# Sums by tensor_reduce, a list that keeps two engines off each other's time, and first-row scores ranked first

## The chip, the cores and the metric

The kernel runs on one core of a Trainium2 chip. The metric is the device time of one execution in microseconds (us). A core has five engines that run their own queues: TensorE (PE in the profile; its weight loads are PEld), VectorE (DVE), ScalarE (ACT), GpSimd (POOL) and SyncE (SP, which here only issues DMAs). They meet through semaphores.

## The reference, cut to what matters

Attention with a threshold comes first, for 8 batches of 8 heads with 576 positions of 64 numbers; then a mixer with a token and a channel part. The mixer's weights are 64-bit floating-point numbers.

```python
scores = (1 / 8) * q @ k.T                       # per batch and head, 576 x 576
thresh = max(scores, axis=-1) - tau
scores = where(scores >= thresh, scores, -1e9)
attn   = exp(scores - max(scores))
attn   = attn / (sum(attn) + 1e-09)
x      = (attn @ v) as (batch, position, head * 64)

h  = relu(x.T @ w_tok1) @ w_tok2                 # tokens:   576 -> 256 -> 576
u  = x + h.T
out = u + relu(u @ w_ch1) @ w_ch2                # channels: 512 -> 1536 -> 512
```

## The kernel before, in words

A **row** is one batch: four pairs of heads. A **unit** is 128 query positions of a pair with both heads, and a **round** is two units. A row has 9 rounds; there are 72 rounds in all, so rounds 0 to 8 are row 0 (in the code `it < UB // 2`, with `UB = 18`).

A round goes through the engines like this. TensorE computes scores of both units into the only two PSUM tiles for scores (`scores_of_two`, L729), so the next round's scores wait for this round's Prelus. VectorE takes four maxima (`top`, L742). GpSimd turns each into a bias (`shift`, L747). ScalarE writes four masked tiles by Prelu (`mask`, L757), then four exponentials with their sums (`exps`, L767; the sum comes out of an accumulator). VectorE adds 1e-9 to the unit's two sums and inverts them (`inverse`, L272 and L273). GpSimd scales the tile by them (`scale`, L280). In row 0 TensorE turns the tile by nine transposes in three banks (`turn`, L295), and VectorE or ScalarE copies each bank out (`turned`, L300); in later rows VectorE and DMAs do the turning (`turn_blocks`, L310, and `move`, L322). TensorE multiplies with the values (`values`, L360 and L365) into a bank that is copied to `xT` (L369). There are four tiles `e`, so a Prelu also waits for the unit four back to be turned. Queries and keys of the next pair are turned by VectorE (`prep`, L265).

The four mixer weights come as 64-bit words and are converted on the chip in 31 pieces: 7 of the token weights, 12 of the first and 12 of the second channel weight. A piece is loaded by a DMA into one of three raw places, ScalarE does two steps (`on_scalar`, L215 and L217), VectorE three (`on_vector`: part 0 at L225, part 1 at L227, part 2 at L231), and GpSimd adds (`on_gpsimd`, L239). Row 0's token part needs the first seven pieces and all of row 0's attention; its channel part needs the others (`ch1` at L834 the first 12, `ch2` at L850 all).

The order on every engine is written before the program runs, by a list (`Scheduler`). An operation has an engine, a planned cost, what it depends on and a rank. For every engine `pick` takes, of the operations that could start by the engine's planned clock, the one of lowest rank, then the oldest; where none could, the earliest. An operation may have an `other` engine with its own cost: whichever picks it first gets it. `start` says from when an operation could run: the planned ends of what it depends on with a lag, a free bank, and the engine's clock. Scores that have rank 1 are also held until as much of the mixer's work has been planned as `planned_at` says.

The ranks that the change touches or passes: scores 1, maxima and biases 0, Prelus 1, conversion steps 1 on ScalarE, 2 on VectorE and 1 on GpSimd, exponentials 2, inverse 2, scaling 1, turns, values and their copies 0, `prep` 3, token steps 1.5. After attention the rest of the channel part runs in a fixed order (L1192 and its neighbours), from about 980 us to the end.

Of the kernel before, what the change touches and what calls it, by code (L numbers as in the profile page):

```python
# [9 lines left out]
F32 = mybir.dt.float32  # L10
# [3 lines left out]
AF = mybir.ActivationFunctionType  # L14
ALU = mybir.AluOpType
AX = mybir.AxisListType

P = 128
# [3 lines left out]
def kernel(  # L22
# [25 lines left out]
    nc = tc.nc  # L48
    B, H, S, D = q.shape
# [19 lines left out]
    const = ctx.enter_context(tc.tile_pool(name="const", bufs=1))  # L69
    work = ctx.enter_context(tc.tile_pool(name="work", bufs=2))  # L70
    small = ctx.enter_context(tc.tile_pool(name="small", bufs=6))
# [15 lines left out]
    UB = 9 * NP // 2  # L87
# [128 lines left out]
            else:  # L216
                nc.scalar.activation(out=h2, in_=hi.bitcast(F32), func=AF.Abs)  # L217

    def on_vector(i, part):
        if wide(i):  # L220
            dst = pieces[i][0]
            lo, hi, h2 = raws[i]
            bits = dst.bitcast(U32)
            if part == 0:
                nc.vector.tensor_scalar(out=h2, in0=h2, scalar1=2.0**-15, scalar2=2.0**16, op0=ALU.max, op1=ALU.mult)  # L225
            elif part == 1:
                nc.vector.tensor_scalar(  # L227
                    out=bits, in0=h2.bitcast(U32), scalar1=3, scalar2=0, op0=ALU.logical_shift_left, op1=ALU.bitwise_or
                )
            else:  # L230
                nc.vector.scalar_tensor_tensor(  # L231
                    out=bits, in0=hi, scalar=0x80000000, in1=bits, op0=ALU.bitwise_and, op1=ALU.bitwise_or
                )
# [13 lines left out]
    tlow = const.tile([P, 1], F32, name="tlow")  # L247
    toff = const.tile([P, 1], F32, name="toff")
    ntau = const.tile([P, 1], F32, name="ntau")


    heads = {}
# [16 lines left out]
    def inverse(u):  # L269
        e, rs = st[u]  # L270
        rr = small.tile([P, 2], F32, tag="rr", name=f"rr_{u}")
        nc.vector.tensor_scalar(out=rr, in0=rs, scalar1=1e-9, scalar2=None, op0=ALU.add)  # L272
        nc.vector.reciprocal(out=rr, in_=rr)  # L273
        st[u] = e, rr

# [212 lines left out]
    class Op:  # L488

        def __init__(self, eng, cost, fn, deps, after, rank, lag, row, index):  # L490
            self.eng, self.cost, self.fn, self.rank, self.lag, self.row, self.index = eng, cost, fn, rank, lag, row, index
            self.end, self.bank, self.frees, self.later, self.open, self.other = None, None, None, [], 0, None
            self.dmas, self.landed = None, None
            self.deps = [d for d in deps if d is not None]
            for d in self.deps + [d for d in after if d is not None]:
                if d.end is None:
                    d.later.append(self)
                    self.open += 1
# [5 lines left out]
    class Scheduler:  # L504
# [5 lines left out]
            self.ready = {e: [] for e in self.clock}  # L510
            self.in_flight, self.moved = deque(maxlen=FLIGHT), 0.0

        def op(self, eng, cost, fn, deps=(), rank=5, lag=0.2, row=None, after=(), other=None, dmas=None):
            x = Op(eng, cost, fn, deps, after, rank, lag, row, len(self.ops))
            x.other, x.dmas = other, dmas
            self.ops.append(x)
            if not x.open:
                self.enter(x)
            return x
# [13 lines left out]
        def start(self, x, eng):  # L533
            t = max([d.landed or d.end + (d.lag if d.eng != eng else 0.0) for d in x.deps] + [0.0])
            if x.dmas and len(self.in_flight) == FLIGHT:
                t = max(t, self.in_flight[0])
            if x.bank:
                frees = [b.free for b in self.banks if b.free is not None]
                if not frees:
                    return None  # L540
                t = max(t, min(frees))
            return max(t, self.clock[eng])
# [68 lines left out]
    sched = Scheduler()  # L611
# [3 lines left out]
    def key_op(*key):  # L615
        return keyed.get(key)

    def put(key, x):
        keyed[key] = x
        return x  # L620
# [17 lines left out]
    def put_dv(i, part):  # L638
        before = key_op("pool", 26) if part == 1 and i >= CONV - 2 else None
        put(  # L640
            ("dv", i, part),
            sched.op(
                "dve",
                (0.46, 0.47, 0.62)[part],
                lambda: on_vector(i, part),
                (key_op("ac", i, 1), key_op("dv", i, part - 1), before),
                CR[2],
            ),
        )

# [64 lines left out]
    def scores_of_two(us):  # L715
        sc = [ps_s2.tile([P, 3, MAIN], F32, tag="sc", name=f"sc{h}_{us[0]}") for h in range(2)]
        for k, u in enumerate(us):
            b, p0, t = units[u]
            if t == SHARED:
                parts = [(b * NP + p0, slice(MAIN, S), slice(0, 64)), (b * NP + p0 + 1, slice(0, LAST), slice(64, P))]  # L720
            else:
                o = P * t if t < SHARED else LAST + P * (t - SHARED - 1)
                parts = [(b * NP + p0 + (t > SHARED), slice(o, o + P), slice(0, P))]
            for f in range(3):
                for n, cols, rows in parts:
                    for h in range(2):
                        r = slice(D * h, D * h + D)
                        qT, kT = heads[n]
                        nc.tensor.matmul(  # L729
                            sc[h][rows, f, HT * k : HT * k + HT],  # L730
                            lhsT=qT[r, cols],
                            rhs=kT[r, HT * f : HT * f + HT],
                            start=True,
                            stop=True,
                            skip_group_check=True,
                        )
            part = [sc[h][:, :, HT * k : HT * k + HT] for h in range(2)]
            st[u] = part, small.tile([P, 2], F32, tag="mx", name=f"mx_{u}"), small.tile([P, 2], F32, tag="bias", name=f"bias_{u}")

    def top(u, h):  # L740
        part, mx, _ = st[u]
        nc.vector.tensor_reduce(out=mx[:, h : h + 1], in_=part[h], axis=AX.XY, op=ALU.max)  # L742

    def shift(u, h):
        _, mx, bias = st[u]
        c = slice(h, h + 1)
        nc.gpsimd.tensor_scalar(out=bias[:, c], in0=mx[:, c], scalar1=toff, scalar2=-SCALE, op0=ALU.add, op1=ALU.mult)  # L747

    def mask(u, h):
        if h == 0:  # L750
            part, _, bias = st[u]
            rs = small.tile([P, 2], F32, tag="rs", name=f"rs_{u}")
            e = att.tile([P, 2 * S], F32, tag="e", bufs=4, name=f"e_{u}")
            masked[u] = e, rs, part, bias
        e, rs, part, bias = masked[u]
        eh = e[:, S * h : S * h + S].rearrange("p (f x) -> p f x", f=3)
        nc.scalar.activation(out=eh, in_=part[h], func=AF.Prelu, bias=bias[:, h : h + 1], scale=SCALE, alpha=STEEP)  # L757
        if h == 1:
            del masked[u]
            st[u] = e, rs  # L760
# [3 lines left out]
    def exps(u, h):  # L764
        e, rs = st[u] if u not in masked else masked[u][0:2]
        eh = e[:, S * h : S * h + S]
        nc.scalar.activation(out=eh, in_=eh, func=AF.Exp, bias=ntau, accum_out=rs[:, h : h + 1])  # L767


    UNITS = len(units)  # L770
# [1 line left out]
    SCORES, VALUES = 2.2, 3.45  # L772
# [202 lines left out]
    def make_round(it):  # L975
        us = (2 * it, 2 * it + 1)
        pre = [key_op("pre", u - 2, h) for u in us for h in range(2)]
        prepared = []
        for u in us:
            b, p0, t = units[u]  # L980
            n = b * NP + p0
            for m in [n] * (t <= SHARED) + [n + 1] * (t >= SHARED):
                prepared += [key_op("prep", m, 0) if it else None, key_op("prep", m, 1)]
                prepared += [key_op("prep", 0, "first")] if not it else []
        x = put(("S", it), sched.op("pe", SCORES, lambda: scores_of_two(us), pre + prepared, 1))
        row, k = divmod(it, UB // 2)
        x.plan = planned_at(row - 1, k) if row else -1.0
        for h in range(2):
            for u in us:
                put(("mx", u, h), sched.op("dve", 0.665, lambda u=u, h=h: top(u, h), (x,), 0))  # L990
                put(("bias", u, h), sched.op("pool", 0.24, lambda u=u, h=h: shift(u, h), (key_op("mx", u, h),), 0))
        for h in range(2):
            for u in us:
                deps = [key_op("bias", u, h)] + [key_op("mx", v_, h) for v_ in us]
                if h == 0:
                    deps += [key_op("T", u - 4), key_op("pre", u - 1, 0)]
                else:
                    deps.append(key_op("pre", u, 0))
                put(("pre", u, h), sched.op("act", 0.64, lambda u=u, h=h: mask(u, h), deps, 1, lag=0.25))
        for u in us:  # L1000
            b, p0, t = units[u]
            for h in range(2):
# [3 lines left out]
            deps = [s]  # L1006
            G = rank_of_group(b, p0, t // GU)
            if not b:
                deps += [key_op("V", G - 2) if t % GU == 0 else None, key_op("T", u - 1)]
                for third in range(3):  # L1010
                    x, y = sched.banked(
                        0.33,
                        lambda bank, u=u, third=third: turn(u, third, bank),
# [8 lines left out]
                    deps = [x]  # L1022
# [348 lines left out]
```

## Time and profile before

| | |
|---|---|
| median of 3 runs | 1346.2 us (1345.57 to 1347.57) |
| the profiled execution | 1346.21 us, its span 1344.3 us |
| mean granted TensorE clock | 0.975 of full speed |
| busy: PE, DVE, ACT, POOL | 1261.7, 802.1, 570.9, 354.2 us |
| conversions on VectorE | 11.6 to 144 us, 93 instructions |
| L272 and L273 (`inverse`) | 144 instructions each, 18.5 to 906 us |
| first token work of row 0's second half | 145.7 us |
| first L834, first L850 | 167.3 us, 206.8 us |

How it is read: busy time is the union of an engine's instructions; the slices cut the span into 40 equal parts; the chain of waits follows the last instruction back to what released it at each step. The timeline lists start, length, engine, line, operation, tiles and shapes, with the idle time before an instruction and its releaser in brackets. A line number is that of the kernel before.

### The profile page before, as it was taken

How to read it: one execution, taken by the hardware profiler on the slowest of the kernel's cores; microseconds unless marked ns; L12 is line 12 of the kernel's file. 1: busy time of each engine (PE TensorE's matmuls, PEld its weight loads, DVE VectorE, ACT ScalarE, POOL GpSimd, SP SyncE). 2: the span in 40 equal slices, each digit the busy share in tenths (PEclk: the TensorE clock that was granted, in tenths of full speed). 3: DMA queues.
4: the chain of work that ended last, by engine and by line, in shares of the span. 5: the costliest groups of instructions: out<-in, count | busy, mean ns of one | idle time of the engine just before them, and what ended most of it. 6: DMA issues, size and time to landing. Idle time of an engine off the chain costs nothing.

```text
span 1344.3 us, 21936 instructions
## 1 busy us (share of the span) xinstructions
PE 1261.7 (94%) x7982; PEld 1002.0 (75%) x7982; DVE 802.1 (60%) x1449; ACT 570.9 (42%) x1244; POOL 354.2 (26%) x658
## 2 busy tenths in 40 slices
PE   6778899999989999998999999899999999999998
PEld 5555579688657866875785776687988888888887
DVE  7899965384756766586576667665154443444352
ACT  6888654464644554455355537541020211112020
POOL 4666522142423323333233323320000000010100
PEclk7798899999989999999999999999999999999999
DMA  9655673463776575675667477173020211021011
GB/s 175 153 137 153 145 166 85 88 153 87 180 168 141 125 161 137 140 155 128 143 157 156 118 154 164 49 180 90 9 69 18 64 32 32 24 58 30 32 32 32
DMA packets 307194, 145.11 MB, mean 108 GB/s; under 512 B 206672, under 2 KB 299856, under 8 KB 307088
## 3 DMA queue, kind: packets, MB, share of 16 engines
q1 hardware_dynamic: 305216, 143.51, 46.3%
q8 instruction: 63, 1.03, 0.3%
q10 hardware_dynamic: 1872, 0.21, 0.1%
q14 instruction: 43, 0.35, 0.1%
HBM read 47.32 MB, written 13.50 MB: 45 GB/s over the span
## 4 chain that ended last, share of the span: by engine, by line
PE 58%; DVE 16%; SPq 10%; ACT 6%; DMA 6%; issue 3%; POOL 1%; DVEq 0%; ACTq 0%; POOLq 0%
PE o L1192 10%; PE bank L850 8%; PE bank L834 7%; SPq L322 6%; DVE mx L742 6%; PE hx L1192 6%; PE bank L365 5%; PE sc L729 5%; PE hz L1192 4%; PE oz L1192 4%; PE hmm L1192 4%; DVE T L310 3%; ACT e L757 3%; ACT e L767 2%; DMA eT<-T 2%
## 5 line engine op out<-in xcount | busy, mean ns | idle before, releaser
L757 ACT ACTIVATE e<-sc,bias 128x576 f32<-128x576 f32 x288 | 197.5, 741 | 223.6 <-DVE mx L742 180.8
L280 POOL TENSOR_SCALAR e<-e,rr 128x576 f32<-128x576 f32 x288 | 211.9, 750 | 284.9 <-DVE rr L273 239.1
L742 DVE TENSOR_REDUCE mx<-sc 128x1 f32<-128x576 f32 x288 | 198.1, 744 | 44.1 <-PE sc L729 44.1
L767 ACT ACTIVATE e<-e,ntau 128x576 f32<-128x576 f32 x288 | 221.0, 779 | 0.2
L310 DVE STREAM_TRANSPOSE T<-e 128x1152 f32<-128x1152 f32 x126 | 171.7, 1369 | 54.4 <-DMA eT<-T 42.3
L729 PE MATMUL sc<-kT,qT 64*128 64x192 f32 (+1 forms) x1920 | 176.4, 345 | 15.8 <-ACT e L757 13.6
L729 PEld LDWEIGHTS sc<-kT,qT 64*128 64x128 f32 (+1 forms) x1920 | 145.7, 183 | 47.9 <-issue 20.3
L850 PEld LDWEIGHTS bank<-wc,g 128*128 128x128 f32 x1536 | 175.0, 192 | 8.5 <-issue 4.9
L850 PE MATMUL bank<-wc,g 128*128 128x128 f32 x1536 | 180.0, 277 | 0.1
L834 PE MATMUL bank<-xT,wc 128*128 128x256 f32 x768 | 177.5, 384 | 0.9 <-DVE g L842 0.7
L834 PEld LDWEIGHTS bank<-xT,wc 128*128 128x128 f32 x768 | 142.4, 190 | 32.6 <-issue 7.5
L365 PE MATMUL bank<-eT,lv 128*64 128x384 f32 (+1 forms) x1024 | 146.5, 431 | 0.0
L747 POOL TENSOR_SCALAR bias<-mx,toff 128x1 f32<-128x1 f32 x288 | 77.7, 273 | 251.2 <-DVE mx L742 249.9
L1275 POOL TENSOR_TENSOR us<-us,ut 128x256 f32<-128x256 f32 x27 | 22.4, 844 | 393.2 <-DVE us L1113 393.2
L365 PEld LDWEIGHTS bank<-eT,lv 128*64 128x64 f32 x1024 | 81.8, 145 | 54.9 <-issue 38.6
L418 PE MATMUL bank<-w,a 128*128 128x288 f32 x256 | 72.4, 426 | 19.9 <-DVE xT L428 18.7
L272 DVE TENSOR_SCALAR rr<-rs 128x2 f32<-128x2 f32 x144 | 42.4, 294 | 68.0 <-ACT e L767 67.5
L418 PEld LDWEIGHTS bank<-w,a 128*128 128x128 f32 x256 | 47.0, 193 | 40.6 <-DVE xT L428 24.5
L406 PE MATMUL bank<-x_sb,w 128*128 128x512 f32 (+1 forms) x180 | 71.3, 549 | 0.6 <-DVE x_sb L398 0.5
L360 PE MATMUL bank<-eT,vl 128*64 128x384 f32 (+1 forms) x256 | 46.9, 444 | 20.1 <-DMA lq<-in_q_dram 3.8
L1240 ACT ACTIVATE ga<-hmm 128x256 f32<-128x256 f32 x30 | 11.5, 384 | 117.1 <-PE hmm L1192 117.1
L1113 DVE TENSOR_TENSOR temps<-hx,temps 128x256 f32<-128x256 f32 x60 | 25.1, 419 | 56.7 <-PE hx L1192 56.6
(128 smaller groups left out, 1552.4 us busy)
## 6 DMA issues: line engine op xcount, KB each, us to landing
eT<-T SPq DMA_DIRECT2D x504, 144.0 KB, 3.0
lk<-in_k_dram SPq DMA_DIRECT2D x126, 72.0 KB, 3.1
lq<-in_q_dram SPq DMA_DIRECT2D x124, 72.0 KB, 3.2
out_dram<-us SPq DMA_DIRECT2D x32, 256.0 KB, 2.1
ut<-us SPq DMA_DIRECT2D x128, 64.0 KB, 2.1
lv<-in_v_dram SPq DMA_DIRECT2D x112, 72.0 KB, 2.5
spare<-in_moe_w_ch_dram SPq DMA_DIRECT2D x8, 512.0 KB, 3.9
extra<-in_moe_w_ch_dram SPq DMA_DIRECT2D x8, 512.0 KB, 3.7
```

Source lines behind the costliest of these rows:

```text
L280: nc.gpsimd.tensor_scalar(out=eh, in0=eh, scalar1=rr[:, h : h + 1], scalar2=1.0, op0=ALU.mult, op1=ALU.mult)
L310: nc.vector.transpose(out=T.rearrange("p a (c x) -> p c a x", c=NK), in_=e.rearrange("p (c a x) -> p c a x", c=NK, a=4))
L322: nc.sync.dma_start(out=turned_e[key][:, place, i, :], in_=T[32 * i : 32 * i + 32])
L365: nc.tensor.matmul(to[r], lhsT=lv[:, j, :], rhs=e[j], start=False, stop=(c == NI - 1), skip_group_check=True)
L418: nc.tensor.matmul(bank[:, 0:HS], lhsT=hidden[b][:, m, P * c : P * c + P], rhs=w2[:, m, HS * f : HS * f + HS], start=(m == 0), stop=(m == ...
L729: nc.tensor.matmul(sc[h][rows, f, HT * k : HT * k + HT], lhsT=qT[r, cols], rhs=kT[r, HT * f : HT * f + HT], start=True, stop=True, skip_gr ...
L742: nc.vector.tensor_reduce(out=mx[:, h : h + 1], in_=part[h], axis=AX.XY, op=ALU.max)
L757: nc.scalar.activation(out=eh, in_=part[h], func=AF.Prelu, bias=bias[:, h : h + 1], scale=SCALE, alpha=STEEP)
L767: nc.scalar.activation(out=eh, in_=eh, func=AF.Exp, bias=ntau, accum_out=rs[:, h : h + 1])
L834: nc.tensor.matmul(bank[:, 0:n], lhsT=wc1[:, j, c, :], rhs=uT[:, c, GR * i : GR * i + n], start=(c == 0), stop=(c == NCC - 1))
L850: nc.tensor.matmul(to, lhsT=s["g"][:, j, P * t : P * t + P], rhs=wc2[:, j, P * c : P * c + P], start=(j == 0 and b > 0), stop=(j == NJ - 1 ...
L1192: nc.tensor.matmul(ps, lhsT=l, rhs=r, start=start and x == 0, stop=x == len(pairs) - 1, skip_group_check=not start)
```

## The change

Three things are done. `inverse` no longer adds 1e-9 by a tensor_scalar: each of eight fixed tiles `sums_of` has 1e-9 beside each of its two sums, written once by GpSimd, the exponentials accumulate into the other places, and a tensor_reduce adds the two. The list gets a mark `shared`: an operation that has it is planned on VectorE no earlier than GpSimd's planned clock; parts 0 and 1 of a conversion have it, and part 0 may go to GpSimd instead, at a planned cost of 0.64. In row 0 scores, maxima, biases and Prelus get rank -1.

```diff
-    def on_vector(i, part):
+    def on_vector(i, part, on=nc.vector):
...
             if part == 0:
-                nc.vector.tensor_scalar(out=h2, in0=h2, scalar1=2.0**-15, scalar2=2.0**16, op0=ALU.max, op1=ALU.mult)
+                on.tensor_scalar(out=h2, in0=h2, scalar1=2.0**-15, scalar2=2.0**16, op0=ALU.max, op1=ALU.mult)
...
+    RS = 8
+    sums_of = [const.tile([P, 2, 2], F32, name=f"rs{i}") for i in range(RS)]
+    for t in sums_of:
+        nc.gpsimd.memset(t[:, :, 1:2], 1e-9)
...
-        nc.vector.tensor_scalar(out=rr, in0=rs, scalar1=1e-9, scalar2=None, op0=ALU.add)
+        nc.vector.tensor_reduce(out=rr, in_=rs, axis=AX.X, op=ALU.add)
...
+            if x.shared and eng == "dve":
+                t = max(t, self.clock["pool"])
...
                 lambda: on_vector(i, part),
                 (key_op("ac", i, 1), key_op("dv", i, part - 1), before),
                 CR[2],
+                other=("pool", 0.64, lambda: on_vector(i, 0, nc.gpsimd)) if part == 0 else None,
+                shared=part < 2,
...
-            rs = small.tile([P, 2], F32, tag="rs", name=f"rs_{u}")
+            rs = sums_of[u % RS]
...
-        nc.scalar.activation(out=eh, in_=eh, func=AF.Exp, bias=ntau, accum_out=rs[:, h : h + 1])
+        nc.scalar.activation(out=eh, in_=eh, func=AF.Exp, bias=ntau, accum_out=rs[:, h, 0:1])
...
-        x = put(("S", it), sched.op("pe", SCORES, lambda: scores_of_two(us), pre + prepared, 1))
+        x = put(("S", it), sched.op("pe", SCORES, lambda: scores_of_two(us), pre + prepared, 1 if it >= UB // 2 else -1))
+        urgent = -1 if it < UB // 2 else 0
...
-                put(("mx", u, h), sched.op("dve", 0.665, lambda u=u, h=h: top(u, h), (x,), 0))
-                put(("bias", u, h), sched.op("pool", 0.24, lambda u=u, h=h: shift(u, h), (key_op("mx", u, h),), 0))
+                put(("mx", u, h), sched.op("dve", 0.665, lambda u=u, h=h: top(u, h), (x,), urgent))
+                put(("bias", u, h), sched.op("pool", 0.24, lambda u=u, h=h: shift(u, h), (key_op("mx", u, h),), urgent))
...
-                put(("pre", u, h), sched.op("act", 0.64, lambda u=u, h=h: mask(u, h), deps, 1, lag=0.25))
+                put(("pre", u, h), sched.op("act", 0.64, lambda u=u, h=h: mask(u, h), deps, urgent or 1, lag=0.25))
```

More of the change, by code (lines that the diff above doesn't have):

```diff
@@ L492, in __init__ @@
             self.end, self.bank, self.frees, self.later, self.open, self.other = None, None, None, [], 0, None
-            self.dmas, self.landed = None, None
+            self.dmas, self.landed, self.shared = None, None, False
             self.deps = [d for d in deps if d is not None]
@@ L511, in __init__, with op @@
             self.in_flight, self.moved = deque(maxlen=FLIGHT), 0.0
-        def op(self, eng, cost, fn, deps=(), rank=5, lag=0.2, row=None, after=(), other=None, dmas=None):
+        def op(self, eng, cost, fn, deps=(), rank=5, lag=0.2, row=None, after=(), other=None, dmas=None, shared=False):
             x = Op(eng, cost, fn, deps, after, rank, lag, row, len(self.ops))
-            x.other, x.dmas = other, dmas
+            x.other, x.dmas, x.shared = other, dmas, shared
             self.ops.append(x)
```

## The prediction

> **What bounds the kernel now.** I read the page's slices first, then busy time by stretch, then the chain of waits for 40 to 154 us, then the timeline of that stretch.
>
> ```profile
> PE   6778899999989999998999999899999999999998
> ...
> DVE  7899965384756766586576667665154443444352
> ACT  6888654464644554455355537541020211112020
> ...
> PEclk7798899999989999999999999999999999999999
> ```
>
> Each digit is a slice of 33.6 us. TensorE (PE) is full from the sixth slice to the end. In the first five it has 6 to 8 tenths at a reduced clock, and there VectorE (DVE) is the fullest. The change works on these slices. Busy time by stretch shows both regimes (PE, PEld, DVE, ACT, POOL, then PE's clock):
>
> ```profile
> 120.00:140.00 20.00, 13.98 (x70) 9.22 (x68) 19.67 (x37) 16.59 (x34) 11.42 (x19) 0.81 0.95 191
> ...
> 200.00:250.00 50.00, 49.93 (x390) 43.62 (x388) 17.93 (x30) 19.30 (x47) 9.69 (x19) 1.00 0.46 103
> ```
>
> PE is idle for 36.5 us of the first 154 (stretches of 40, 20, 20, 20, 20, 20 and 14 us: idle 11.5, 6.6, 4.0, 4.9, 1.9, 6.0, 1.5), 36 us from 336 to 900, and almost never after that. Since PE's backlog is unbroken from about 170 to 336 us, what brings the early stretch to its end sooner moves the end of the kernel by about as much.
>
> The chain of waits for 40 to 154 us (first its shares, then start, length, engine and line):
>
> ```profile
> by line: DVE mx L742 13.6%; DVE wc L227 12.1%; DVE wc L231 9.7%; issue 8.0%; PE bank L295 7.0%; DVE rr L272 6.1%; DVE high L225 5.7%; PE sc L729 5.3%; DMA extra<-in_moe_w_ch_dram 4.4%; PE bank L365 3.4%; DVE eT L300 2.8%; POOL e L280 2.6%;
> ...
> 102.06 1.41 DVE wc L227
> ...
> 137.84 1.19 DVE rr L272
> ```
>
> VectorE carries it, and two of its lines are far longer than their work. L272 adds 1e-9 to two numbers; L227 shifts 512 words:
>
> ```profile
> L272 DVE TENSOR_SCALAR rr<-rs x144: 117/169/1261, 18.5 to 905.2; 128x2 f32<-128x2 f32 x144
> ```
>
> The timeline shows why:
>
> ```profile
> 101.61 0.42 DVE L225 TENSOR_SCALAR high<-high 128x512 f32<-128x512 f32 x1
> ...
> 101.83 1.35 POOL L239 TENSOR_TENSOR wc<-wc,spare 128x512 int32<-128x512 int32 x1 [2.54 <-DVE wc L231]
> ...
> 102.06 1.40 DVE L227 TENSOR_SCALAR wc<-high 128x512 uint32<-128x512 uint32 x1
> ...
> 137.69 1.29 POOL L239 TENSOR_TENSOR wc<-wc,spare 128x512 int32<-128x512 int32 x1 [1.53 <-issue]
> 137.75 1.26 DVE L272 TENSOR_SCALAR rr<-rs 128x2 f32<-128x2 f32 x1
> ```
>
> L227 takes 0.42 us when GpSimd (POOL) is quiet. Here it lasts until 103.46, 0.28 us after L239 ends at 103.18. L272 takes 0.16 us when free; here it ends 0.03 us after L239. A VectorE tensor_scalar that starts while GpSimd runs waits for GpSimd's end.
>
> **The change, part by part.** The profiled execution took 1346.21 us (span 1344.3 and 1.9 around it), the median of three runs is 1346.2, so sums are made on 1346.2.
>
> *The sum by tensor_reduce.* 144 instructions change form. The 120 that start after 160 us take 32.3 us, against 19.2 at 0.16 each: 13.1 us of waiting. The 24 before take 10.1 against 3.8: 6.3 us. The new form is in no row of this trace. Its fixed part is bounded below by the shortest L272 (0.12 us) and above by the reciprocal next to it plus a little (0.166, say 0.20); I take 0.16, the free L272, so the instruction's own work changes by nothing (bounds -6 to +6 us of VectorE time over the kernel, under 1 us of it in the early stretch). Whether it waits for GpSimd is bounded by L272 (as before) and by L742, a tensor_reduce that reads PSUM, at 719 to 758 ns whatever GpSimd does. I take no wait, as the operation is the same as L742's. On the chain from 40 to 154 us L272 has six long pieces (1.19, 1.01, 1.27, 1.00, 1.19 and 0.43 us); less 0.16 each that is 5.1 us. The Trainium skill, "SBUF — State Buffer", section "Who interferes with whom", states that on trn2 tensor_reduce never contends for the port pair that VectorE shares with GpSimd; no run here shows it for an SBUF source. By that rule the 5.1 us go; by the L272 row nothing goes. After 154 us the chain holds eleven pieces of 0.55 to 0.62 us: 4.6 us above the free duration. But there the scaling of the next unit is queued behind GpSimd's own first scaling (L280, 0.75 us each), which an earlier inverse does not hurry, so I take 2 (bounds 0 and 5). The eight memsets of 128x2 lie in GpSimd's idle time from 3 to 9.7 us; uncovered they would cost 0.8 (0.10 each) to 2.5 (0.31 each).
>
> *The list and the shared time.* On the chain from 40 to 154 us nine L227 pieces are longer than 0.43: 1.40, 0.86, 0.79, 1.40, 1.41, 1.41, 1.41, 1.42, 0.79, together 7.0 us too long. L225 adds 1.0. The list now plans parts 0 and 1 of a conversion at GpSimd's clock or later, and other VectorE work goes first. But it plans with its own costs, it doesn't hold GpSimd back while VectorE runs, and it leaves part 2 (L231) out. L231 waits as well:
>
> ```profile
> 142.13 1.42 POOL L239 TENSOR_TENSOR wc<-wc,spare_a 128x512 int32<-128x512 int32 x1 [1.53 <-DVE high L225]
> ...
> 142.44 1.67 DVE L231 SCALAR_TENSOR_TENSOR wc<-extra,wc 128x512 uint32<-128x512 uint32 x1
> ```
>
> It takes 0.69 free, and 1.4 us of the chain is this wait, which stays. The same page says that an instruction with two SBUF inputs contends with a GpSimd one that reads SBUF; L231 agrees, and it speaks against the list's marking of only two parts. Of the 8.0 us I take half as avoided (bounds 0 and 8).
>
> So 5.1 + 4.0 = 9.1 us leave the VectorE chain. Next late is ScalarE, with 16.6 us busy of 20 in the row above, so I credit two thirds: **-6** (bounds 0 and -13).
>
> *Part 0 on GpSimd.* It may move there when GpSimd is free earlier. The nearest row is L280, 0.75 us for 576 elements of the same operation: 0.67 for 512, against 0.42 on VectorE. GpSimd is busy 98 of the first 168 us; all 31 pieces would add 20. Each moved one brings a wait for ScalarE's L217 into GpSimd's queue, with biases (L747) and scalings (L280) behind it, for which Prelus and turns wait, and a handover to L227 of some 0.4 us (the gap before L747). I take **+1**, bounds -2 and +5.
>
> *Row 0 first.* Scores, maxima, biases and Prelus of rounds 0 to 8 pass ahead of turns, copies and conversions. Between the fourth maximum and the last Prelu's end an undisturbed round takes 161.68 - 159.50 = 2.2 us, and round 5 takes 74.24 - 68.84 = 5.4:
>
> ```profile
> 67.43 1.41 DVE L742 TENSOR_REDUCE mx<-sc 128x1 f32<-128x576 f32 x2
> ...
> 72.27 1.97 ACT L757 ACTIVATE e<-sc,bias 128x576 f32<-128x576 f32 x3
> ...
> 156.75 2.75 DVE L742 TENSOR_REDUCE mx<-sc 128x1 f32<-128x576 f32 x4 [0.45 <-PE sc L729]
> ...
> 160.31 1.37 ACT L757 ACTIVATE e<-sc,bias 128x576 f32<-128x576 f32 x2
> ```
>
> In between ScalarE runs four conversion steps of 0.67 us, an exponential and two copies. Over the nine rounds it is 35.8 us where 19.8 would do: 16.0 us that the rank can take back. Not all will show: exponentials keep their rank behind the conversions, a Prelu needs the tile of the unit four back to be turned, and the transposes of the next pair (L265) keep rank 3: round 6's scores stood still for 2.0 us for one. The conversions pay, but they can: their last step ends at 145.5, the first use of the second weight (L850) is at 206.8. SP's queue only sees the conversions' loads later; the q and k loads have theirs behind them no more than now. I take 40%: **-6.5** (bounds +3 and -16).
>
> Sum: 1346.2 - 6 - 2 + 1 - 6.5 = 1332.7, so **1333**. The list also orders the later rows anew; their 36 us of idle PE may move by 5 either way, taken as 0. Own range 1323 to 1342.
>
> **Rivals.** *More:* all 13.1 us of waits and the 16 us of Prelus come back, row 0's second half of tokens (first at 145.7 us) starts near 120, and PE is full from there: 1346 - 28 = 1318. For it: 36.5 us of idle PE and the clock of 0.8 that goes with it. Against: ScalarE.
>
> *No net:* the waits go, and the same time is spent waiting for exponentials and GpSimd, since VectorE's next order is no better: 1346.
>
> *Slower:* the conversions starve. Part 1 waits for GpSimd, which now has bias, scaling, the adds and part 0, and row 0 is ahead of them everywhere. Today a piece comes every 4.4 us (135 us for 31). Beyond 6.3 us a piece the last one comes after 206 us, and PE waits for its L850 work, microsecond for microsecond. At 7.0 it ends at 227: 20 us of idle PE, against some 9 won before: 1357. Against it: even with all of part 0 GpSimd would be busy 118 of the first 168 us.
>
> **How the numbers follow.** Measurement tells 0.2% (2.7 us) from no change. Forecast 0.60 (0.58 faster, 0.02 same); more 0.14; no net 0.08 (0.02, 0.05, 0.01); slower 0.18. Together faster 0.74, same 0.07, slower 0.19. The range reaches half-way into both rivals, 1314 to 1355, with about 0.07 left below and 0.10 above.
>
> **What would show it.** Right: the new form at 0.12 to 0.20 us beside a running L239 or L280; half of the L227 under 0.5 us; round 8's Prelus end before 110 us (now 117); row 0's last values (L365, 143.5) before 134; PE idle in the first 154 us under 28. Wrong: the new form at 1.2 us; L239's last beyond 200; idle PE between 336 and 900 over 45 us, which would be the later rows' order and not row 0.

## The result and the profile after

The changed kernel takes 1336.11 us (median of 6 runs, 1328.56 to 1337.61) against 1345.88 beside it: a ratio of 0.9918, 95% interval 0.9898 to 0.9939. That is 9.8 us less (forecast: 13). The profiled execution took 1337.61 us, its span is 1335.8; it is the slowest of the six, at the lowest granted TensorE clock (0.977, the others 0.980 to 0.987).

The page's slices, of 33.4 us now:

```profile
PE   6878999989899998998999999999999999999998
...
DVE  5887893474746666577477667565054443444442
...
POOL 5987872232323332333233324320000000000100
PEclk7988999999999999999999999999999999999999
```

GpSimd's line of the kernel before:

```profile
POOL 4666522142423323333233323320000000010100
```

VectorE has 5 to 8 tenths in the first four slices, where it had 7 to 9. GpSimd, which had 4 to 6, has 5 to 9: it is now the fullest engine in the second and the third, and over the first 154 us as a whole. TensorE is little better off. Busy time of the first 154 us, before and after (PE, PEld, DVE, ACT, POOL, then PE's clock):

```profile
0.00:154.00 154.00, 117.55 (x749) 82.75 (x750) 137.30 (x256) 117.58 (x242) 91.22 (x149) 0.84 0.67 148
```

```profile
0.00:154.00 154.00, 120.85 (x802) 85.19 (x803) 117.24 (x230) 111.54 (x232) 121.90 (x172) 0.88 0.63 137
```

VectorE is 20 us less busy, GpSimd 31 us more. TensorE's idle time fell by only 3.3 us, to 33.2. The sum's line shows the first part of the change at work (minimum, median and maximum in ns), and part 0's lines show what went wrong with the list's option:

```profile
L276 DVE TENSOR_REDUCE rr<-rs x144: 105/156/174, 23.4 to 896.6; 128x2 f32<-128x4 f32 x144
```

```profile
L225 POOL TENSOR_SCALAR high<-high x26: 1060/1924/2419, 15.7 to 182.1; 128x512 f32<-128x512 f32 x22, 128x288 f32<-128x288 f32 x3, 64x256 f32<-64x256 f32 x1
L225 DVE TENSOR_SCALAR high<-high x5: 427/860/1277, 14.5 to 181.5; 128x512 f32<-128x512 f32 x4, 128x288 f32<-128x288 f32 x1
```

Of 144 sums none waits any more. Of 31 parts 0, 26 moved to GpSimd, at 1.92 us for 512 elements where the list had planned 0.64. The timeline shows what that does to a round of row 0:

```profile
61.45 0.50 POOL L755 TENSOR_SCALAR bias<-mx,toff 128x1 f32<-128x1 f32 x2
...
61.75 1.37 ACT L765 ACTIVATE e<-sc,bias 128x576 f32<-128x576 f32 x2 [1.81 <-POOL bias L755]
...
61.91 1.92 POOL L225 TENSOR_SCALAR high<-high 128x512 f32<-128x512 f32 x1
...
63.81 0.77 POOL L755 TENSOR_SCALAR bias<-mx,toff 128x1 f32<-128x1 f32 x2
63.87 0.43 DVE L227 TENSOR_SCALAR wc<-high 128x512 uint32<-128x512 uint32 x1 [1.39 <-POOL high L225]
...
64.38 1.37 ACT L765 ACTIVATE e<-sc,bias 128x576 f32<-128x576 f32 x2 [1.25 <-POOL bias L755]
```

The third and fourth bias stand behind part 0 in GpSimd's queue, ScalarE's Prelus wait for them, and VectorE waits for part 0 itself. In the waits of the first 170 us (who waited for whom, us, times, longest) the Prelu's line was 5.4 us before and is now second of all:

```profile
ACT e L757 <- POOL bias L747: 5.4, 4, 2.4
```

```profile
ACT e L765 <- POOL bias L755: 15.6, 13, 2.0
```

Where the 8.5 us of span come from: TensorE's idle time fell from 82.6 to 79.1 us (3.3 in the first 154 us, 1.6 up to 200, 2.3 from 350 to 900; from 200 to 350 it rose by 3.6), and its busy time from 1261.7 to 1256.7. Its work is the same, so the clock is the likely cause: 68 us of the span were at half speed before, 61 after. That is worth at most half of 7.6 us, 3.8 of the 5.0; the rest is not explained. Row 0 ends much earlier (its last values product at 121.2 us, 143.5 before), but the conversions end at 194.4 us in place of 145.5, and the first L858 (the second weight's product) starts with them.

### The profile page after: what moved, and what is told of

It is laid out like the page before. It is cut to its first block, busy times and chain, and to the rows that moved or that the text cites. A ratio compares the mean times of both kernels' runs of the same rounds, so it can differ in the third digit from the quotient of the medians.

```text
span 1335.8 us, 21934 instructions
## 1 busy us (share of the span) xinstructions
PE 1256.7 (94%) x7982; PEld 997.6 (75%) x7982; DVE 774.2 (58%) x1429; ACT 568.1 (43%) x1238; POOL 404.2 (30%) x692
## 4 chain that ended last, share of the span: by engine, by line
PE 57%; SPq 12%; DVE 11%; DMA 6%; ACT 5%; POOL 5%; issue 3%; DVEq 0%; ACTq 0%; POOLq 0%
PE o L1201 10%; PE bank L858 7%; PE bank L842 7%; SPq L326 6%; PE hx L1201 6%; PE sc L737 5%; PE bank L369 5%; DVE mx L750 5%; PE hz L1201 4%; PE oz L1201 4%; PE hmm L1201 4%; SPq L106 4%; DVE T L314 3%; ACT e L765 2%; DMA lv<-in_v_dram 2%
## 5 line engine op out<-in xcount | busy, mean ns | idle before, releaser
L737 PE MATMUL sc<-kT,qT 64*128 64x192 f32 (+1 forms) x1920 | 176.7, 343 | 13.5 <-ACT e L765 11.7
L858 PEld LDWEIGHTS bank<-wc,g 128*128 128x128 f32 x1536 | 175.0, 192 | 8.1 <-issue 3.8
L858 PE MATMUL bank<-wc,g 128*128 128x128 f32 x1536 | 179.7, 276 | 0.0
L369 PE MATMUL bank<-eT,lv 128*64 128x384 f32 (+1 forms) x1024 | 138.5, 411 | 0.1
L369 PEld LDWEIGHTS bank<-eT,lv 128*64 128x64 f32 x1024 | 76.6, 138 | 51.1 <-issue 37.4
L422 PE MATMUL bank<-w,a 128*128 128x288 f32 x256 | 77.2, 449 | 21.5 <-DVE xT L432 21.3
L422 PEld LDWEIGHTS bank<-w,a 128*128 128x128 f32 x256 | 49.9, 204 | 44.2 <-DVE xT L432 27.4
L276 DVE TENSOR_REDUCE rr<-rs 128x2 f32<-128x4 f32 x144 | 21.2, 148 | 68.5 <-ACT e L775 68.3
L775 ACT ACTIVATION_READ_ACCUMULATOR e<-e,ntau 128x1 f32 x288 | 58.8, 204 | 0.0
```

The costliest lines, as they stand in the source:

```text
L369: nc.tensor.matmul(to[r], lhsT=lv[:, j, :], rhs=e[j], start=False, stop=(c == NI - 1), skip_group_check=True)
L422: nc.tensor.matmul(bank[:, 0:HS], lhsT=hidden[b][:, m, P * c : P * c + P], rhs=w2[:, m, HS * f : HS * f + HS], start=(m == 0), stop=(m == ...
L737: nc.tensor.matmul(sc[h][rows, f, HT * k : HT * k + HT], lhsT=qT[r, cols], rhs=kT[r, HT * f : HT * f + HT], start=True, stop=True, skip_gr ...
L858: nc.tensor.matmul(to, lhsT=s["g"][:, j, P * t : P * t + P], rhs=wc2[:, j, P * c : P * c + P], start=(j == 0 and b > 0), stop=(j == NJ - 1 ...
```

## The experiments

Theory A is that each part of the change does its own work and that part 0's time on GpSimd takes much of it back. Its rivals stand with each run. All ratios are against the kernel before on the same chip, with 95% intervals. For comparing them, a hundredth is 13.5 us.

**The tensor_reduce alone** (the kernel before, with its order, plus `sums_of` and the tensor_reduce).

```diff
...  (sums_of and its memsets)
-        nc.vector.tensor_scalar(out=rr, in0=rs, scalar1=1e-9, scalar2=None, op0=ALU.add)
+        nc.vector.tensor_reduce(out=rr, in_=rs, axis=AX.X, op=ALU.add)
...  (exps accumulates into sums_of)
```

> The kernel before with the tensor_reduce alone; the order on every engine stays as it was. Theory A (each part of the change does its own work): the sum no longer waits for GpSimd, all 144 under 0.2 us; of the 5.1 us of its waits on the chain from 40 to 154 us and the 4.6 us after, two thirds and two fifths come back: 1346 - 3.4 - 2 = 1340 to 1342. Theory B (the whole gain of the change is this wait): 1335 to 1338. Theory C (these waits lie beside other work): 1345 to 1347.

Measured: 1337.45 against 1341.61 us, ratio 0.9971 (0.9953 to 0.9989), some 4 us. No sum waits, and row 0's last values end at 138.8 us, 4.7 earlier. This is theory A's size, and it rules out that the sum's wait is all of the change's gain.

**The ranks alone.**

```diff
-        x = put(("S", it), sched.op("pe", SCORES, lambda: scores_of_two(us), pre + prepared, 1))
+        x = put(("S", it), sched.op("pe", SCORES, lambda: scores_of_two(us), pre + prepared, 1 if it >= UB // 2 else -1))
+        urgent = -1 if it < UB // 2 else 0
...  (maxima, biases and Prelus with urgent)
```

> The kernel before with the ranks of row 0 alone. Theory A: row 0's second half of tokens starts some 10 us before 145.7, conversions end later than 146 but before 170, time 1338 to 1342. Theory B (only the sum's wait counts): 1344 to 1348. Theory D (the ranks alone push inverse and conversions back, so that VectorE's waits for GpSimd eat it): 1346 to 1352.

Measured: 1342.06 against 1341.61 us, ratio 1.0002 (0.9983 to 1.0020): nothing. Row 0's last values end at 139.1 us, only 4 earlier, and the sum's addition waits more:

```profile
L272 DVE TENSOR_SCALAR rr<-rs x24: 152/410/1341, 22.8 to 163.9; 128x2 f32<-128x2 f32 x24
```

Its median in the first 168 us is 410 ns, where it was 164. So A's number for the ranks was wrong, and the mechanism of D (waits eat it) is seen, although the time is no worse. It is not the whole of it. Over rounds 0 to 7 the time from the fourth maximum to the last Prelu, which the ranks are to shorten, sums to 19.6 us in place of 30.5; in round 8 alone it is 15.7 in place of 5.3:

```profile
96.99 2.74 DVE L742 TENSOR_REDUCE mx<-sc 128x1 f32<-128x576 f32 x4
...
102.90 0.16 DVE L272 TENSOR_SCALAR rr<-rs 128x2 f32<-128x2 f32 x1
...
110.86 0.87 PE L295 MATMUL bank<-ident,e 128*128 128x128 f32 x6 [0.99 <-DVE xT L428]
...
111.83 1.37 ACT L757 ACTIVATE e<-sc,bias 128x576 f32<-128x576 f32 x2
```

Round 8's Prelus write the tiles `e` of round 6, and start only once these are turned. Round 6's last exponential ended at 95.5 us, its first sum was added at 102.9, behind round 8's maxima and steps of two conversions (in the kernel before: 91.3 and 91.6).

**The list's mark with the option, alone.**

```diff
+            if x.shared and eng == "dve":
+                t = max(t, self.clock["pool"])
...
+                other=("pool", 0.64, lambda: on_vector(i, 0, nc.gpsimd)) if part == 0 else None,
+                shared=part < 2,
```

> The kernel before with the list's mark and GpSimd's option for part 0, without the tensor_reduce and the ranks. In the changed kernel 26 of 31 parts 0 ran on GpSimd at 1.92 us each for 512 elements, planned at 0.64. Theory A: VectorE's waits at part 1 go, but GpSimd is 40 us busier and its biases and scalings late: 1346 to 1352, conversions end after 170. Rival (GpSimd has the room, as the prediction took it): 1338 to 1343.

Measured: 1337.89 against 1341.61 us, ratio 0.9973 (0.9957 to 0.9988). By its number the rival held, and A had taken the loss for larger than what the mark brings. The mechanism was A's all the same: 24 of the parts 0 ran on GpSimd, at 1.92 us for 512 elements, and the conversions ended at 184.6 us. What the option costs in this order is told by the mark alone, further down: 0.9973 against 0.9901, some 10 us.

**The changed kernel with part 0 kept on VectorE.**

```diff
-                other=("pool", 0.64, lambda: on_vector(i, 0, nc.gpsimd)) if part == 0 else None,
                 shared=part < 2,
```

> The changed kernel with part 0 kept on VectorE: tensor_reduce, ranks and the mark stay, GpSimd has no option. Theory A: GpSimd's queue is 36 us shorter (26 x 1.4 us over the VectorE price), conversions end near 150 in place of 194, biases no longer wait behind part 0, and the time is 1326 to 1332. Rival (the mark holds VectorE's conversions back behind GpSimd just as well, or the load was hidden): 1334 to 1339.

Measured: 1312.81 against 1341.61 us, ratio 0.9784 (0.9757 to 0.9811). It is the best kernel of the study, and below A's range. Against the changed kernel's 0.9918 the option had cost 0.0134, or 18 us. The conversions still end late, at 188.3 us, so A's 150 is wrong: it isn't part 0 alone that holds them. The mark does: without it they end at 142 to 159 us in all runs, with it and VectorE's steps at rank 2 at 179 to 217. The first 154 us of it, for the two lines above:

```profile
0.00:154.00 154.00, 131.26 (x926) 94.73 (x928) 131.15 (x279) 127.41 (x268) 92.57 (x172) 0.96 0.72 161
```

TensorE is idle for 22.7 us there (33.2 with the option, 36.5 before), at a clock of 0.96.

**Part 0 on GpSimd without the clamp.** To tell the place from the duration, the changed kernel keeps the list's inputs, and with them its order and its 26 moved parts, but GpSimd multiplies twice; the clamp at 2**-15 is left out there.

```diff
-                on.tensor_scalar(out=h2, in0=h2, scalar1=2.0**-15, scalar2=2.0**16, op0=ALU.max, op1=ALU.mult)
+                on.tensor_scalar(
+                    out=h2, in0=h2, scalar1=2.0**-15 if on is nc.vector else 1.0, scalar2=2.0**16,
+                    op0=ALU.max if on is nc.vector else ALU.mult, op1=ALU.mult,
+                )
```

> The changed kernel in its own order, with part 0 as two multiplications (by 1 and by 2**16) wherever GpSimd runs it: the clamp at 2**-15 is left out there, which changes weights that are smaller. Theory A (what went wrong with part 0 is its duration on GpSimd): 0.66 to 0.70 us each in place of 1.92, as the scaling's row has it, and the time 1316 to 1326. Rival 1 (it is the place, GpSimd's queue order with its waits): durations fall and the time stays 1332 to 1337. Rival 2 (GpSimd is slow on this tile whatever the operation): still 1.9 us.

```profile
L225 POOL TENSOR_SCALAR high<-high x26: 397/617/1107, 15.1 to 167.8; 128x512 f32<-128x512 f32 x22, 128x288 f32<-128x288 f32 x3, 64x256 f32<-64x256 f32 x1
```

Measured: 1316.58 against 1343.87 us, ratio 0.9802 (0.9785 to 0.9820). The same tile takes 0.62 us, and 15.6 of the 18 us are back; the interval overlaps that of the kernel without the option, so the rest may be noise. So it was the duration, and the duration is that of a maximum followed by a multiplication.

**The mark alone**, part 0 on VectorE.

> The kernel before with the mark alone: part 0 and 1 are planned at GpSimd's clock or later, on VectorE. Theory A: most of the 14 us of waiting at part 1 goes, conversions end by 170, time 1334 to 1339 (4 to 8 us less than before on the same chip). Rival (without ranks and tensor_reduce the wait turns up at the sum's addition, whose instances then wait more often): within 2 us of before.

Measured: 1329.0 against 1343.87 us, ratio 0.9901 (0.9880 to 0.9923): 13 us, well beyond A; the conversions end later than A's 170. The 26 shifts of 512 words sum to 13.7 us where they were 23.3, so 9.6 of 12.4 us of waiting went. Row 0's last values end at 119.1 us in place of 143.5, the conversions at 180. The rival's mechanism is there as well, in the first 168 us:

```profile
L272 DVE TENSOR_SCALAR rr<-rs x27: 148/544/1278, 18.0 to 166.8; 128x2 f32<-128x2 f32 x27
```

The sum's addition waits for 17.6 - 27 x 0.16 = 13.3 us there, against 6.3 before. The mark pays in spite of it.

**Tensor_reduce and ranks**, without the mark.

> The kernel before with tensor_reduce and ranks, without any of the list's mark. Ranks alone gave nothing, and in that run the sum's addition waited more (14.8 us for 24 in the first 168 us, 10.4 for 26 before). Theory A (the parts help each other: the ranks' gain had been eaten by that wait): 8 to 14 us less than before on the same chip. Rival (parts add up: 4 and 0): 3 to 5 us less. If the mark is what makes the ranks pay, this run is no better than tensor_reduce alone.

Measured: 1334.3 against 1343.87 us, ratio 0.9929 (0.9910 to 0.9949), 9.6 us: A. The ranks, worth nothing alone, are worth some 5 or 6 us beside the tensor_reduce (0.9929 against 0.9971 on another chip; the intervals just miss each other). Round 8's step from the fourth maximum to the last Prelu still takes 14.9 us, so that loss is not the wait for GpSimd.

**Tensor_reduce and mark**, without the ranks.

> The kernel before with tensor_reduce and mark (part 0 on VectorE), without the ranks. The mark alone was worth 1.0%, the tensor_reduce alone 0.3%, all three without GpSimd's option 2.2%. Theory A (the ranks pay once VectorE has room, although alone they gave nothing): 1.3 to 1.6% less than before, 1322 to 1326 where before is 1343. Rival (the ranks never pay, mark and tensor_reduce help each other): 2.0 to 2.3% less, 1313 to 1316.

Measured: 1319.8 against 1344.32 us, ratio 0.9821 (0.9795 to 0.9846), between the two ranges. That is 24 us, where the two alone gave 4 and 13: they help each other. With the ranks it was 0.9784, and the intervals overlap: whether the ranks pay there stays open.

**The measured price in the list.**

```diff
-                other=("pool", 0.64, lambda: on_vector(i, 0, nc.gpsimd)) if part == 0 else None,
+                other=("pool", 1.95, lambda: on_vector(i, 0, nc.gpsimd)) if part == 0 else None,
```

> The changed kernel with the measured cost for part 0 on GpSimd in the list: 1.95 in place of 0.64, the option stays. Theory A (the list was misled by the price): it takes the option less often, GpSimd's plan fits what runs, 1315 to 1328. Rival (the list has no notion of what waits behind GpSimd, so it takes it as often as GpSimd is free): still 20 or more of 31 on GpSimd and 1330 to 1340.

Measured: 1329.08 against 1344.32 us, ratio 0.9890 (0.9866 to 0.9914). 21 parts still go to GpSimd, as the rival said; the time lies a microsecond outside both ranges. An operation goes to whichever engine can start it first, and the price isn't asked in that choice (`pick` compares start, rank and age); it only moves GpSimd's planned clock.

Three tries to better the best kernel failed, each in the way its rival named, the second by more than its rival had allowed. **Mark on part 2 too** (`shared=part < 3`):

> The changed kernel with part 0 on VectorE and the mark on part 2 too, whose waits for GpSimd stayed (up to 1.1 us in the run without GpSimd's option). Theory A: part 2 waits less, but its waits came to only some 1 us in all there, so 1309 to 1314. Rival (holding part 2 as well strings the conversion on GpSimd's idle times and it ends after 200 us): 1316 to 1325.

Measured: 1322.13 against 1343.87 us, ratio 0.9840 (0.9821 to 0.9859). The conversions end at 197.1 us, and TensorE is idle for 10 us between 168 and 200.

**Row 0's exponentials ahead of the conversions** (rank 0.5 in place of 2):

> The version with part 0 on VectorE (1312.8) with row 0's exponentials at rank 0.5, ahead of ScalarE's conversion steps. Theory A (row 0 now waits for exponentials that queue behind conversions: up to 10 us from the last Prelu to the last exponential of a round): row 0's second half of tokens starts 5 to 10 us before 120, and 1304 to 1311. Rival (the conversions are the bound by now: they end at 188, where the second weight's first use waits for them): their end moves past 195 and 1313 to 1322.

Measured: 1331.59 against 1344.32 us, ratio 0.9919 (0.9898 to 0.9939). Row 0's second half of tokens started at 114.6 us, the earliest of all, and the last conversion ended at 217.2:

```profile
215.88 1.29 POOL L239 TENSOR_TENSOR wc<-wc,extra 128x512 int32<-128x512 int32 x1 [1.31 <-ACT e L774]
```

The second weight's first product followed at 221.5, and TensorE was idle for 18 us from 168 to 250. The rival's upper end, 1322, was nearly 10 us too low. This is the mechanism of the prediction's slower rival, at work on a kernel that is still faster than before.

**VectorE's conversions further ahead** (rank -0.5 in place of 2):

> The version with part 0 on VectorE with VectorE's conversion steps at rank -0.5: behind row 0's maxima, ahead of later rows' and of copies. Theory A (there TensorE idles 5 us between 168 and 200 because the conversions end at 188): they end by 170, and 1306 to 1311. Rival (copies and turns behind them hold TensorE in row 0): 1314 to 1325.

Measured: 1324.55 against 1344.32 us, ratio 0.9862 (0.9835 to 0.9889). The conversions end at 164.8 us, as A had it, but row 0's last values only at 125.1 (110.6 in the best), and TensorE is idle for 33 us in the first 154.

## Why the prediction was right, and where its steps were wrong

The direction, the place and the range held: the early stretch ended sooner and the end of the kernel followed. But the sum was right by luck: two errors of opposite sign.

Nor did the end move "by about as much", as the prediction's premise had it. Row 0's last values came 22 us earlier and its second half of tokens 17, the kernel's end 10. The kernel with tensor_reduce and mark ends row 0 at the same 121 us as the changed one and is some 13 us faster. What the conversions and the clock do after it counts as well.

*Part 0 on GpSimd* was taken at +1 us with -2 and +5 as bounds. It cost about +18 (0.9918 against 0.9784). The step that failed is "The nearest row is L280, 0.75 us for 576 elements of the same operation": L280 multiplies twice, part 0 takes a maximum and multiplies. The same engine, form and tile take 0.62 us with the one and 1.92 with the other. A row of the same instruction but another operation was no bound; its upper end had to be open. With the duration that the prediction had assumed, the place itself costs little: at 0.62 us the kernel is 2.4 us from the one without the option (0.9802 against 0.9784, the intervals overlap), inside the bounds.

*The gains* were taken at -14.5 without that term and measured -29 (0.9784). The terms, one by one:
- The tensor_reduce: no wait, 0.156 us in the median (taken: 0.16, bounds 0.12 and 0.20). Forecast 3.4 + 2 = 5.4 us, alone 4 (0.9971), with row 0 ending 4.7 us sooner. This was right; no run shows the 2 us after 154 us apart. The rule of the Trainium skill ("SBUF — State Buffer", "Who interferes with whom") that a tensor_reduce never contends on trn2 is now shown here for an SBUF source: 144 of 144 within 174 ns, while GpSimd ran beside 63 of them.
- The mark: forecast half of 8.0 us, two thirds of that credited, 2.7. Alone it gave 13 (0.9901). More of the wait went than half (9.6 of 12.4 us at part 1), but that is hardly all: the mark seems to work as a rank too. The list lets other VectorE work go first while GpSimd is busy, so row 0 ended 24 us earlier, and the conversions 35 us later, into slack that the prediction had seen (L850 at 206.8) and credited to the ranks alone. No run parts the two effects; that taking the conversions forward again by rank (164.8 us) costs the best kernel 10 us fits it.
- The ranks: forecast 6.5, alone nothing. The step that failed is "I take 40%": in rounds 0 to 7 the ranks took back 10.9 of the 16.0 us, and round 8 lost 10.4 again, waiting for the tiles of round 6. The prediction had named this bound ("a Prelu needs the tile of the unit four back to be turned") and priced it too low. With the tensor_reduce in place about 5.6 us more appear, which fits inverses that no longer wait for GpSimd. In the changed kernel itself the step from the fourth maximum to the last Prelu took 33.5 us over row 0's nine rounds, 2.3 less than the 35.8 before; without the option it is 24.9, or 10.9 less, and with part 0 at 0.62 us 27.2. The prediction's 40% of 16.0 us is between, and most of the difference is the long part 0 in front of the biases.
- The parts don't add: alone 4, 0 and 13 us, together 29. VectorE waited at three places for the same engine, and freeing one moved part of the wait to the next: with the mark alone the sums waited 7 us more, with the tensor_reduce alone parts 0 and 1 took 2.2 us longer (42.6 against 40.4).

*The clock* was in no term, only in the rival "more". It may be nearly half of what came: from before to the best kernel TensorE's idle time falls by 18.6 us (82.6 to 64.0) and its busy time for the same work by 14.8 (1261.7 to 1246.9), with half-speed time in the span falling from 68 to 34 us. These are two executions. Over all runs on the best kernel's chip the median granted clock is 0.977 before and 0.987 in the best; at 2 x (1 - clock) of the span that is an estimate of 62 and 34 us at half speed, worth at most 14 of the 29 us.

Of the signs named beforehand: the new form at 0.12 to 0.20 us beside a running GpSimd (0.105 to 0.174: right); half of the 31 parts 1 under 0.5 us (right: 8 of the 26 long ones are above, 15 before); round 8's Prelus before 110 us (103.8: right); row 0's last values before 134 (121.2: right); TensorE idle under 28 us in the first 154 (33.2: wrong, and here the loss to GpSimd showed); L239's last beyond 200 as a sign of failure (194.4: close); idle time from 336 to 900 over 45 us (34.1: not so).

## What to carry to other kernels

Price a moved operation from a row of the same operation on the same engine, not only of the same instruction and shape; where there is none, run it once. Where a list lets an engine take an operation because it is free first, its cost there must enter the choice, or the option is better left out. Waits for a shared resource are worth removing at all the places where they can turn up: the tensor_reduce and the mark gave 4 and 13 us alone, together 24. Before ranking work first, ask which buffers it needs and who frees them: the ranks alone shortened their step by 11 us in eight rounds and lost 10 in the ninth.

## What the runs showed of the hardware that was not expected

- GpSimd's tensor_scalar on 128x512 float32 takes 1.92 us as maximum and multiplication and 0.62 us as two multiplications. VectorE takes 0.42 for the first. The Trainium skill ("GPSIMD Engine Reference", section 4.1) calls one-input elementwise work on GpSimd, a maximum among it, roughly line-rate; for a maximum with a multiplication these runs disagree; no run has a maximum alone.
- The granted clock is part of the price of idle time on TensorE. In the kernel before 48 us of the first 200 were at half speed, in the changed one 38, with the mark alone 20, in the best 17. The Trainium skill ("TensorE: Matmul & The Clock Gate", "What's actually happening") says that a clock gate halves the clock after an idle window of about 3.4 us and releases it after a busy one. The traces agree in that half-speed stretches inside the span are 3.4 us or multiples of it and follow idle time. They differ in that no window need be idle throughout: of the 3.4 us ahead of each such stretch TensorE was idle for 1.4 to 3.4 in the kernel before and 1.7 to 3.3 in the best, and twice before for only 1.4 of the last 6.8. What starts one was not tried, and the total of idle time doesn't tell it: the mark alone and tensor_reduce with ranks leave TensorE idle for 79.1 us each, at 20 and 38 us of half speed in the first 200.
- GpSimd loses time as well: a bias of 0.26 us took up to 1.0 in the changed kernel (at 167.34 us, until 0.05 us after VectorE's L227 ended), and VectorE's two-input step of the conversion (L231) still took up to 1.8 us, where 0.69 is its free time.
